# Neural codec with residual quantisation on one core: a tighter rule for which x transposes and which adding DMAs may be in flight together

## The chip, the cores and the metric

The kernel runs on one core of one Trainium2 chip. The metric is the device time of one execution in microseconds. The kernel before took 708.34 us in the median of three runs (700.25 to 710.99).

## The reference

The input x has 2 sequences of 16000 tokens with 512 channels, in bf16. A depthwise convolution with 3 taps over time and a SiLU give z. Then four codebooks of 8 words each quantise z in turn, each on what the one before has left over. The sum of the chosen words goes through a second depthwise convolution with 3 taps.

```python
xp = jnp.pad(x, ((0,0),(pad,pad),(0,0)))
for i in range(K):
    z = z + xp[:, i:i+T, :] * dw_enc[i][None, None, :]
z = _silu(z)
res = z
for s in range(Nq):
    cb = codebooks[s]
    d2 = |res|^2 - 2.0 * einsum("btd,cd->btc", res, cb) + |cb|^2
    sel = cb[d2.argmin(-1)]
    q = q + sel
    res = res - sel
...
    y = y + qp[:, i:i+T, :] * dw_dec[i][None, None, :]
```

## The kernel before

The 32000 tokens stand as 128 partitions of 250 tokens. They are worked in 16 chunks of up to 16 token positions each (`SIZES`). For a chunk the work is done with channels on the partitions, so x has to be transposed: chunk 0 is transposed by TensorE, and each of the 15 others by five DMA transposes, issued on SyncE (SP) by `run` at L544. Four of them bring four positions each and the last one two; the last chunk has four of them and one single row, `edge` at L550. That makes 75 transposes. They fill `XT`, which has two buffers, so a chunk's transposes can begin when the chunk two before has been read for the last time.

In `front`, each of four channel blocks of a chunk makes three products of `XT` with a tap on VectorE (DVE, L614): one into `Z` (four buffers), two into `T` (four buffers). The products have to be summed. For the chunks after the first, `DMA_ADDS` says that the first sum of every block and the second sum of the last block are made by a DMA that adds `T` into `Z` (`total`, L620), issued on GpSimd (POOL); DVE makes the other sums (L622). That makes 15 x 5 = 75 adding DMAs. When an add has landed, its `T` buffer is free for a later product, and `Z` may be summed further or go to the exponential on ScalarE (ACT, L626). SiLU follows as exponential, plus one, logarithm, exponential and product.

The stages after that (scores on TensorE, maxima and keys on DVE, the choice, the new residue) and the decoder do not change. A finished block of output leaves as `YSB` (three buffers) by a DMA on SP (L908), so the stores and the transposes share one queue of instructions.

The order of everything is set beforehand by a planner (`Plan`): it simulates the engines with estimated costs and emits the instructions of all engines in one order. Its "DMA" engine issues one transfer at a time and may delay a change between the two kinds (`APART`, `CLUMP`). Each engine then works through its own instructions in that order and waits at semaphores. Beside the waits that the data ask for, `keep_apart` adds one to each transpose and to each add: a transpose waits for the landing of the last but one add emitted before it, and an add for that of the last but one transpose (`LAG = 2`). The plan does not know of these waits.

In the order of emission the transposes (R) and the adds (A) stand like this:

```
RRRRRRRARARAARARAARARRRARAAARRRARARRARAARRAARARRRARAAARAR
RRARAAARARRRAARAARARRARARAAARRRRAARAARARRRAARAARARRAARARA
RARRRARAAARARARARARARARRRRAAAAAAAAAA
```

Of the kernel before, what the change touches and what calls it, by code (L numbers as in the profile page):

```python
# [57 lines left out]
LAG = 2  # L58
# [151 lines left out]
def kernel(  # L210
# [181 lines left out]
    def pair_rows(s):  # L392
        pst = psA.tile([P, 2, 512], F32, name="ps_p", tag="psa")
        for k, src in ((0, CBC), (1, CB4)):
            nc.tensor.matmul(pst[:, k, :], lhsT=PICK[k][:, s, :, :, :].rearrange("p h a b -> p (h a b)"), rhs=src[0:NC, :],
                             start=True, stop=True)
        nc.scalar.activation(HIGH[s], pst[:, 0, :], ACT.Copy, scale=-1.0)
        nc.scalar.activation(EVEN[s], pst[:, 1, :], ACT.Copy, scale=-1.0)
# [21 lines left out]
    for name, first, tap, count in (("A0", 0, 1, 2), ("A1", 0, 0, 3), ("A2", 1, 0, 3), ("A3", 2, 0, 2),  # L420
                                    ("B0", 3, 0, 1), ("B3", 0, 2, 1), ("A2LO", 1, 0, 1)):
        t = const.tile([P, D], BF16, name=name)
# [35 lines left out]
    for s in range(Nq - 1):  # L458
        t = plan.add("ACT", 1.1, 1.5, [picked, clamped, book], early + 3.0 + s, lambda s=s: pair_rows(s), take=("psA",), give=("psA",))
# [1 line left out]
    codes.append(plan.add("DVE", 1.4, 1.6, [codes[0]], 0.1 * PERIOD, lambda: code_columns(RESB[1])))  # L461
    gate, decoder = [], []
    staged = [*words, scored[1], taps_in]
    runs, adds = [], []

    def keep_apart(t, mine, others):
        if len(others) >= LAG:
            tc.add_manual_dep(t.ins, others[-LAG].name, mybir.DependencyInfo(mybir.DependencyClass.Sync, mybir.DependencyReason.DATA),
                              reason="transposes and adds take turns")
        mine.append(t.ins)  # L470

# [59 lines left out]
    def load(st, org):  # L531
# [10 lines left out]
        def run(n, m):  # L542
            g = g0 + n - 1
            t = nc.sync.dma_start_transpose(out=st["XT"][:, n:n + m, :, :].rearrange("p n i t -> p (n i) t"),  # L544
                                        in_=xv[:, g:g + m, :].rearrange("p g d -> p (g d)"))
            keep_apart(t, runs, adds)

        def edge(n):
            st["XE"] = const.tile([P, KT, P], BF16, name="XE")
            keep_apart(nc.sync.dma_start_transpose(out=st["XE"], in_=group_rows(0)), runs, adds)  # L550
# [35 lines left out]
    def front(st, org):  # L586
# [19 lines left out]
        def block(i):  # L606
# [10 lines left out]
            def total(k):  # L617
                z, t = u["Z"][:, 0:G, :], u["ZTU"[k]][:, 0:G, :]
                if i in DMA_ADDS[st["n"]][k - 1]:
                    keep_apart(nc.gpsimd.dma_start(out=z, in_=t, accum_op=ALU.add), adds, runs)  # L620
                else:
                    nc.vector.tensor_tensor(out=z, in0=z, in1=t, op=ALU.add)  # L622
# [380 lines left out]
```

## Time and profile before

| | |
|---|---|
| median of three runs | 708.34 us (700.25 to 710.99) |
| profiled execution, its own time | 703.44 us |
| its span, first to last instruction | 701.6 us |
| mean granted TensorE clock | 0.952 |
| busy: PE / DVE / ACT / POOL | 572.6 / 628.1 / 616.2 / 85.5 us |
| DMA queue of SP (transposes, stores) | 69.61 MB, 45.9% of 16 engines' span |
| DMA queue of POOL (adds) | 39.76 MB, 32.3% |
| an add, issue to landing, median | 6.0 us |
| a transpose, issue to landing, median | 6.6 us |

A busy time is that of an engine's own work; an instruction that only issues a DMA does not count as work on SP. A line of a group gives the line of the kernel, the engine, the operation, what is written and read, the number of instructions, then the busy time with the mean of one, then the idle time of the engine just before them and what ended it. SPq and POOLq are the queues' own issuing and waiting. A wait for several semaphores is put down to the one that came last.

### The profile page before, as it was taken

Reading aid. Unit: us, or ns where it says so; the run is one execution under the profiler, and the core shown is the slowest. Engines: PE = TensorE matmul, PEld = TensorE weight load, DVE = VectorE, ACT = ScalarE, POOL = GpSimd, SP = SyncE. Lnnn points to the kernel's source line nnn. Section 1 sums busy time; section 2 is a strip of 40 time slices with the busy share of each in tenths; the row PEclk is TensorE's granted clock in tenths of the full one; section 3 lists DMA queues with packets and bytes.
Section 4 is the critical chain, followed back from the end, with each engine's and each line's share of the span. In section 5 each row is a group of like instructions: output and inputs, shape, how many; then the busy total and the mean of one; then the engine's idle time right before and its main releaser. Section 6 shows DMA issues by size and latency. Waiting matters only on the chain. (4 is left out here: it accounts for less than half of the span.)

```text
span 701.6 us, 25642 instructions
## 1 busy us (share of the span) xinstructions
PE 572.6 (82%) x11501; PEld 328.9 (47%) x11582; DVE 628.1 (90%) x1292; ACT 616.2 (88%) x519; POOL 85.5 (12%) x120
## 2 busy tenths in 40 slices
PE   5136778898988988899929788898989987999995
PEld 5023444454545545445515444464545554565552
DVE  8999999999999999999939799999999999968640
ACT  2789999999999999999939888999999999963567
POOL 6021111100101111101101111010112002000000
PEclk8559999999999999999979989999999999999999
DMA  7999997997797999799999959979998536210235
GB/s 161 155 179 169 159 174 154 183 215 144 174 175 177 168 215 187 174 172 185 158 81 199 183 104 182 183 183 184 189 171 174 143 92 163 78 66 33 82 141 230
DMA packets 160840, 111.27 MB, mean 159 GB/s; under 512 B 142425, under 2 KB 142810, under 8 KB 160602
## 3 DMA queue, kind: packets, MB, share of 16 engines
q1 hardware_dynamic: 148976, 69.61, 45.9%
q0 software_dynamic: 11472, 39.76, 32.3%
q8 instruction: 90, 1.47, 0.9%
q10 hardware_dynamic: 282, 0.26, 0.1%
q14 instruction: 20, 0.16, 0.1%
HBM read 2.39 MB, written 32.77 MB: 50 GB/s over the span
## 5 line engine op out<-in xcount | busy, mean ns | idle before, releaser
L710 PE MATMUL PS<-RES 128*64 128x72 bf16 (+1 forms) x8064 | 173.5, 201 | 30.5 <-DVE RES L314 16.7
L710 PEld LDWEIGHTS <-RES 128*64 128x64 bf16 x8064 | 168.8, 113 | 39.0 <-DVE RES L642 18.4
L846 DVE TENSOR_TENSOR RES<-RES,SEL 128x2048 bf16<-128x2048 bf16 (+1 forms) x135 | 153.6, 1152 | 7.0 <-PE SEL L836 6.4
L864 ACT ACTIVATE RES<-NEW 128x1024 bf16<-128x1024 f32 x114 | 118.9, 1075 | 23.2 <-PE NEW L857 22.9
L904 ACT ACTIVATE YSB<-Y 128x1024 bf16<-128x1024 f32 (+1 forms) x126 | 126.6, 1052 | 14.1 <-issue 3.6
L620 POOL DMA_DIRECT2D Z<-T x75 | 72.3, 968 | 494.9 <-DVE V L753 51.2
L626 ACT ACTIVATE E<-Z 128x2048 bf16<-128x2048 bf16 (+1 forms) x64 | 123.2, 1927 | 7.6 <-DVE Z L622 3.2
L634 ACT ACTIVATE LN<-E 128x2048 f32<-128x2048 bf16 (+1 forms) x64 | 123.9, 1936 | 6.5 <-DVE E L630 6.4
L637 ACT ACTIVATE E<-LN 128x2048 bf16<-128x2048 f32 (+1 forms) x64 | 123.6, 1931 | 0.2
L614 DVE TENSOR_SCALAR T<-XT,WENC 128x2048 bf16<-128x2048 bf16 (+1 forms) x128 | 93.7, 738 | 20.8 <-DMA Z<-T 20.1
L730 DVE TENSOR_REDUCE TR<-PS 128x6 bf16<-128x384 f32 (+1 forms) x188 | 94.2, 507 | 18.4 <-PE PS L710 18.2
L852 PE MATMUL NEW<-RES,IDENT 128*128 128x512 bf16 (+1 forms) x252 | 76.4, 386 | 17.5 <-DVE RES L846 10.7
L898 PE MATMUL Y<-A,OHT 128*128 128x512 bf16 x205 | 74.5, 383 | 11.7 <-ACT YSB L904 3.3
L642 DVE TENSOR_TENSOR RES<-Z,E 128x2048 bf16<-128x2048 bf16 (+1 forms) x64 | 76.7, 1198 | 0.6 <-PE PS L710 0.4
L702 PE MATMUL PS<-MASK,IDENT 128*64 128x384 bf16 (+1 forms) x376 | 63.0, 331 | 5.5 <-DVE PR L734 3.4
L622 DVE TENSOR_TENSOR Z<-Z,T 128x2048 bf16<-128x2048 bf16 (+1 forms) x53 | 62.3, 1176 | 2.3 <-DMA Z<-T 2.3
L836 PE MATMUL SEL<-PH,HIGH 64*128 64x512 bf16 (+1 forms) x258 | 51.0, 389 | 15.9 <-ACT RES L864 5.8
L857 PE MATMUL NEW<-PH,EVEN 64*128 64x256 bf16 (+1 forms) x252 | 53.4, 420 | 0.0
L898 PEld LDWEIGHTS <-OHT 128*128 128x128 bf16 x373 | 31.7, 98 | 43.4 <-issue 16.9
L857 PE MATMUL NEW<-PH,HIGH 64*128 64x256 bf16 (+1 forms) x252 | 49.4, 388 | 2.9 <-ACT PH L809 2.9
L836 PE MATMUL SEL<-PH,LOW 64*128 64x512 bf16 (+1 forms) x258 | 49.3, 373 | 0.0
L836 PE MATMUL SEL<-PH,MID 64*128 64x512 bf16 (+1 forms) x258 | 49.2, 373 | 0.0
(111 smaller groups left out, 591.3 us busy)
## 6 DMA issues: line engine op xcount, KB each, us to landing
Z<-T POOLq DMA_DIRECT2D x75, 512.0 KB, 6.0
out_dram<-YSB SPq DMA_DIRECT2D x61, 512.0 KB, 4.5
RES<-in_x_dram SPq DMA_DIRECT2D x1, 1664.0 KB, 6.8
XT<-in_x_dram SPq DMA_TRANSPOSE x74, 6.6
out_dram<-YSB SPq DMA_DIRECT2D x1, 384.0 KB
out_dram<-YSB SPq DMA_DIRECT2D x1, 256.0 KB, 2.9
A<-in_dw_dec_dram POOLq DMA_DIRECT2D x2, 96.0 KB, 9.6
CB<-in_codebooks_dram ACTq DMA_DIRECT2D x1, 128.0 KB
```

The costliest lines, as they stand in the source:

```text
L614: nc.vector.tensor_scalar(out=places(u[name]), in0=taps(i, k), scalar1=WENC[:, i, k:k + 1], scalar2=None, op0=ALU.mult)
L626: nc.scalar.activation(u["E"][:, 0:G, :], u["Z"][:, 0:G, :], ACT.Exp, scale=-1.0)
L634: nc.scalar.activation(u["LN"][:, 0:G, :], u["E"][:, 0:G, :], ACT.Ln)
L637: nc.scalar.activation(u["E"][:, 0:G, :], u["LN"][:, 0:G, :], ACT.Exp, scale=-1.0)
L710: nc.tensor.matmul(V[d * HT:(d + 1) * HT, own - left:own + HT + right], lhsT=row[:, at:at + HT], rhs=row[:, at - left:at + HT + right], st ...
L730: nc.vector.tensor_reduce(out=to, in_=both(u["V", q], m, home, HT), axis=AX.X, op=ALU.max)
L836: nc.tensor.matmul(SEL[:, h, 0:W], lhsT=words[side(h), i * P:(i + 1) * P], rhs=u["PH"][side(h), :], start=(k == 0), stop=(k == len(parts) ...
L846: nc.vector.tensor_tensor(out=old, in0=old, in1=new, op=ALU.add)
L857: nc.tensor.matmul(odd[:, h, k, 0:W // 2], lhsT=words[side(h), i * P:(i + 1) * P], rhs=pairs[side(h)], start=False, stop=True, skip_group_ ...
L864: nc.scalar.activation(old, new.rearrange("p h (n t) -> p (h n) t", t=HT), ACT.Copy)
L898: nc.tensor.matmul(Y[:, h, :], lhsT=lhs(), rhs=rhs, start=(a == 0), stop=(a == len(terms) - 1))
L904: nc.scalar.activation(u["YSB"][:, k:k + n, :], u[k][:, 0:n, :], ACT.Copy)
```

## The change

`keep_apart` now remembers which kind came last. The first transpose after an add still waits for the last but one add, and the first add after a transpose for the last but one transpose. Each further one of the same kind in a row waits for the last of the other kind. Thus of the 75 + 75 waits, 24 of transposes and 30 of adds now name a transfer that is one later. The plan, the order on each engine and all other waits are as before.

```diff
-    runs, adds = [], []
+    runs, adds, turns = [], [], []
 
     def keep_apart(t, mine, others):
-        if len(others) >= LAG:
-            tc.add_manual_dep(t.ins, others[-LAG].name, mybir.DependencyInfo(mybir.DependencyClass.Sync, mybir.DependencyReason.DATA),
+        lag = LAG if turns[-1:] == [id(others)] else 1
+        turns.append(id(mine))
+        if len(others) >= lag:
+            tc.add_manual_dep(t.ins, others[-lag].name, mybir.DependencyInfo(mybir.DependencyClass.Sync, mybir.DependencyReason.DATA),
                               reason="transposes and adds take turns")
         mine.append(t.ins)
```

## The prediction

> **What bounds the kernel now.** I read the page first: busy shares, the slices, then the two groups that the change can reach.
>
> ```profile
> span 701.6 us, 25642 instructions
> PE 572.6 (82%) x11501; PEld 328.9 (47%) x11582; DVE 628.1 (90%) x1292; ACT 616.2 (88%) x519; POOL 85.5 (12%) x120
> DVE  8999999999999999999939799999999999968640
> ...
> L620 POOL DMA_DIRECT2D Z<-T x75 | 72.3, 968 | 494.9 <-DVE V L753 51.2
> ...
> L614 DVE TENSOR_SCALAR T<-XT,WENC 128x2048 bf16<-128x2048 bf16 (+1 forms) x128 | 93.7, 738 | 20.8 <-DMA Z<-T 20.1
> ```
>
> VectorE (DVE) is busy nine tenths of every slice but the ends and one hole: slice 21 of 40, about 351 to 368 us, is at 3. The product L614 idles 20.8 us, and 20.1 of it ends on an adding DMA. Next, DVE's waits between 31 and 600 us (engine, line, releaser: sum, times, longest), then two stages of the table by stage (us; busy of PE, PEld, DVE, ACT, POOL; granted clock; DMA share; GB/s).
>
> ```profile
> DVE T L614 <- DMA Z<-T: 20.1, 6, 12.6
> DVE TR L730 <- PE PS L710: 2.8, 7, 0.8
> DVE Z L622 <- DMA Z<-T: 2.3, 3, 1.0
> ...
> 210.00:300.00 90.00, 79.67 (x1696) 46.10 (x1707) 88.72 (x182) 87.89 (x75) 11.43 (x13) 1.00 0.88 183
> ...
> 345.00:370.00 25.00, 12.66 (x275) 7.66 (x271) 12.43 (x25) 14.31 (x11) 0.86 (x1) 0.80 0.98 92
> ```
>
> So an undisturbed stage runs DVE at 88.72 of 90 us. What DVE loses in mid-kernel it loses to adds that land late: 20.1 + 2.3 = 22.4 us in nine waits. All other waits there are small. The DMA share in the bad stage is 0.98 at half the usual GB/s: the engines were occupied and moved little.
>
> **The change part by part.** No instruction is added, removed or reordered; only what a transpose (SP, L544) or an add (POOL, L620) waits for. In the sequence shown above, 54 waits move on by one member: 24 transposes and 30 adds, each the second or later of its row. I number both kinds from 0.
>
> *The adds' 30 new waits.* Each is for the last transpose of the row before, when one for the last but one is already met. In the profiled order those transposes left long before the add did, so I cost these at nothing. The cover is the earlier add of the row, at 968 ns of issue, and the products that DVE makes between the two; without it, each would cost what a late transpose costs below.
>
> *The hole.* Timeline rows (start, length, engine) around it, then time to landing of the add at 343.67 and of the transpose at 348.12, then the same over all adds from 31 to 343 us and from 370 to 600 us:
>
> ```profile
> 343.19 4.88 SPq L544 DMA_TRANSPOSE XT<-in_x_dram  x1
> 343.67 0.86 POOL L620 DMA_DIRECT2D Z<-T  x1 [5.38 <-DVE PR L734]
> 348.12 14.29 SPq L544 DMA_TRANSPOSE XT<-in_x_dram  x1
> 362.76 0.75 DVE L614 TENSOR_SCALAR T<-XT,WENC 128x2048 bf16<-128x2048 bf16 x1 [12.57 <-DMA Z<-T]
> ...
> DMA to landing us min/median/max: 19.1/19.1/19.1
> DMA to landing us min/median/max: 16.6/16.6/16.6
> ...
> DMA to landing us min/median/max: 4.5/6.0/8.3
> DMA to landing us min/median/max: 4.5/6.4/9.3
> ```
>
> Add 44 is issued 0.48 us behind transpose 51; transpose 52, second in its row, joins at 348.12. The add takes 19.1 us, and DVE, ready at 362.76 - 12.57 = 350.19, stands until it lands, for want of a T buffer. After the change transpose 52 waits for add 44. Bounds for the add beside transpose 51 alone: 6.0 us (median) to 9.3 (longest elsewhere), so it lands between 349.7 and 353.0 and DVE waits 0 to 2.8 us: a saving of 9.8 to 12.57. Lower bound: no saving, if transpose 51 alone did it (a rival below). I take 11, since every other add with a transpose beside it stays inside 9.3.
>
> *Two smaller stalls.*
>
> ```profile
> 393.12 1.47 POOL L620 DMA_DIRECT2D Z<-T  x1 [6.93 <-DVE PR L734]
> 393.96 6.65 SPq L544 DMA_TRANSPOSE XT<-in_x_dram  x1
> 400.90 0.75 DVE L614 TENSOR_SCALAR T<-XT,WENC 128x2048 bf16<-128x2048 bf16 x1 [4.92 <-DMA Z<-T]
> ...
> 197.81 0.75 DVE L614 TENSOR_SCALAR T<-XT,WENC 128x2048 bf16<-128x2048 bf16 x1 [1.45 <-DMA Z<-T]
> ```
>
> Transpose 57 (393.96), third of its row, comes right behind add 49 (393.12). Without it the add lands at 6.0 us, 399.1, not 400.9: saves 1.8 (0 to 3.3, by the 4.5 minimum). At 197.81 the third-in-row transpose only started as the add landed: nothing. The remaining waits, 22.4 - 12.57 - 4.92 - 1.45 = 3.5 us, have one transpose or none beside them: nothing.
>
> *What the waiting transposes cost.* Eight of the 24 had not been clear of the add by the profile: numbers 13, 27, 37, 46, 52, 57, 62, 72. The others left when that add was down or within half a us of it. First and last of the eight, each behind its add:
>
> ```profile
> 71.52 0.86 POOL L620 DMA_DIRECT2D Z<-T  x1 [6.61 <-DVE PR L734]
> 72.87 5.77 SPq L544 DMA_TRANSPOSE XT<-in_x_dram  x1
> ...
> 516.60 0.86 POOL L620 DMA_DIRECT2D Z<-T  x1 [6.12 <-DVE MT L791]
> 520.92 2.57 SPq L544 DMA_TRANSPOSE XT<-in_x_dram  x1
> ```
>
> With the 6.0 us median the first waits 71.52 + 6.0 - 72.87 = 4.65 us, the last 1.7; the eight together about 25 us, or 25 + 8 x 3.3 = 51 with the longest landing, 9.3. Little of this is lost. DMA packets, us 234 to 236.5 (an add, q0, beside a transpose, q1), then 238 to 241 (transposes alone):
>
> ```profile
> q0 software_dynamic: 129, 0.47, 94.3%
> q1 hardware_dynamic: 142, 0.03, 6.2%
> ...
> q1 hardware_dynamic: 2607, 0.65, 98.5%
> ```
>
> While the add's data moves, transposes get 142 / 2.5 = 57 packets a us; alone 2607 / 3 = 869. A transpose that waits its turn gives up a fifteenth of its speed. What it truly loses is the start from landing to first packet, once per place.
>
> Then, who waits for it. On SP the stores stand behind it; on POOL the next row's first add, which waits for the last transpose but one; on DVE the first product of the chunk. SP's waits, POOL's wait, the last transpose of a chunk (418.65, 8.5 to landing) with that chunk's first product, and add 29, transpose 37 and the add behind it:
>
> ```profile
> SPq L908 <- ACT YSB L904: 165.3, 35, 16.6
> SPq L544 <- DMA Z<-T: 95.9, 23, 9.5
> POOL Z L620 <- DMA XT<-in_x_dram: 14.9, 3, 11.6
> ...
> 418.65 4.85 SPq L544 DMA_TRANSPOSE XT<-in_x_dram  x1
> DMA to landing us min/median/max: 8.5/8.5/8.5
> 433.59 0.74 DVE L614 TENSOR_SCALAR T<-XT,WENC 128x2048 bf16<-128x2048 bf16 x1
> ...
> 230.31 0.86 POOL L620 DMA_DIRECT2D Z<-T  x1 [5.16 <-DVE E L630]
> 233.37 4.65 SPq L544 DMA_TRANSPOSE XT<-in_x_dram  x1
> 242.04 0.86 POOL L620 DMA_DIRECT2D Z<-T  x1 [10.87 <-DVE V L753]
> ```
>
> SP sits idle 165.3 us for output tiles, so stores have cover. This chunk lands at 418.65 + 8.5 = 427.2 and is first read at 433.59: 6.4 us of slack, more than the 5.2 us of the longest single wait. The adds are the thin place. Transpose 37 would leave at 230.31 + 6.0 = 236.3, or at 238.6 with the 8.3 us of the longest landing up to then; with 4.65 us of issue it is done by 243 or so, against 242.04 for the add behind it: 1 us late. I take 1 us for all such places together (the other waits end before DVE's inputs for the add are ready). Bounds: -1, if freed adds also start sooner, to 25, if every wait reaches DVE.
>
> *The sum.* On the profiled execution, 703.44 us (span 701.6 and 1.8 around it): - 11 - 1.8 + 1 = - 11.8, so 691.6. That execution lies 4.9 below the median of 708.34 (runs 700.25 to 710.99). I take the median run to carry more of the same stalls and let half of the 4.9 stay: 691.6 + 2.4 = 694.
>
> A rule of the Trainium skill speaks against the 11: in "DMA: Bandwidth & Descriptors", section "Queues, rings and completion order", each DMA engine takes turns between its queues packet by packet. By it a second transpose in the same queue takes no extra turns from the add, and the sum would lose its first term and most of its second: about 704. The rows at 234 us agree with it (142 packets beside 129); the hole, where one add took 19.1 us, does not look like it.
>
> **The rivals.**
>
> *The stall stays.* What slowed add 44 is transpose 51, ahead of it since 343.19 and still allowed beside it. For it: DMA was already slow before 348.12 (110 GB/s from 346 to 349), and in the queues transpose 52 stands behind 51. Against it: most other adds have one transpose beside them and none exceeds 9.3 us. Then only the 1.8 goes and 1 comes: 702.6, or nothing gained if a stall falls elsewhere: 702, up to 708.
>
> ```profile
> 346.00:349.00 3.00, 3.00 (x84) 1.86 (x79) 3.00 (x9) 3.00 (x4) 0.00 (x0) 1.00 1.41 110
> 349.00:362.00 13.00, 3.06 (x71) 1.81 (x65) 1.19 (x2) 5.53 (x5) 0.00 (x0) 0.81 1.20 65
> ```
>
> *Slower: transposes held behind adds hold the next adds.* One chain: add lands, transpose leaves, next row's add waits for it, DVE waits for that add. It decides where a transpose's new wait exceeds the add's room, about 1 us at the place above. If the eight waits, 25 us, reach DVE and the savings stand: 691.6 + 25 = 717, and 720 with the 2.4. For it: 23 transpose waits on adds already exist, and POOL lost 14.9 us to transposes. Against: the speeds of 57 and 869 above, and 6.4 us at the chunk's edge.
>
> *All the add stalls go.* If relief shortens every late add, DVE's 22.4 us vanish: 703.44 - 22.4 + 2.4 = 683.
>
> *It does nothing.* 46 of 54 waits are already met; if the other eight also sit inside slack and the hole is chance, the time is that of before, 703 to 708. I put it with the first rival.
>
> **How the numbers follow.** No change cannot be told from a difference under about 2% here, so the lines are 694.2 and 722.5. Forecast 694: chance 0.48, its own range 687 to 700, just over half of it (0.25) below 694.2. Stall stays or nothing: 0.22, 702 to 708. Slower: 0.18, 709 to 735, two thirds (0.12) above 722.5. All stalls go: 0.12. Faster by over 2%: 0.25 + 0.12 = 0.37. Slower: 0.12. Within: the remaining 0.51. The range 684 to 712 leaves out half of the last case and most of the slower one, together under 0.2.
>
> **What would show it.** Right: the longest L620 time to landing falls from 19.1 to under 10, DVE's L614 wait on adds falls from 20.1 us to about 8, the DMA-starved slice 21 fills, and SP's L544 waits on adds rise from 95.9 us by about 25. Wrong: an add still takes over 12 us with only one transpose beside it (the stall stays), or POOL's waits on transposes and DVE's on adds both grow (slower).

## The result: 0.7% slower, and the profile after

Over 20 runs each, the changed kernel takes 710.66 us in the median (706.57 to 716.56), the kernel before 706.87 (700.25 to 716.74). The ratio is 1.0068, with a 95% interval of 1.0042 to 1.0094: 3 to 7 us slower, where 14 us faster had been forecast. Executions more than 1.5% above the fastest of their kernel are left out of the ratios and their intervals here and below, so a ratio differs a little from the quotient of the medians (here 1.0054). The profiled execution after took 707.11 us, before 703.44.

The page after, its lines that answer to those of before (line numbers of the changed part are two higher):

```profile
span 705.3 us, 25642 instructions
PE 578.1 (82%) x11501; PEld 332.0 (47%) x11582; DVE 629.1 (89%) x1292; ACT 616.8 (87%) x519; POOL 86.3 (12%) x120
...
DVE  8999998999989999999939799999999999868640
...
L616 DVE TENSOR_SCALAR T<-XT,WENC 128x2048 bf16<-128x2048 bf16 (+1 forms) x128 | 93.9, 740 | 19.7 <-DMA Z<-T 19.7
```

The hole in DVE is where it was, slice 21 at 3. DVE's waits between 31 and 600 us say the same (sum, times, longest):

```profile
DVE T L616 <- DMA Z<-T: 19.7, 4, 12.9
DVE Z L624 <- DMA Z<-T: 4.2, 3, 3.2
```

19.7 + 4.2 = 23.9 us against 22.4 before. The stall is as deep as ever, although its suspect is gone. The rows of the timeline around it (start, length, engine), with the time to landing of the add:

```profile
344.79 4.90 SPq L546 DMA_TRANSPOSE XT<-in_x_dram  x1
345.28 0.86 POOL L622 DMA_DIRECT2D Z<-T  x1 [5.38 <-DVE PR L736]
364.72 2.20 SPq L546 DMA_TRANSPOSE XT<-in_x_dram  x1
364.73 0.75 DVE L616 TENSOR_SCALAR T<-XT,WENC 128x2048 bf16<-128x2048 bf16 x1 [12.94 <-DMA Z<-T]
...
DMA to landing us min/median/max: 19.4/19.4/19.4
```

Transpose 52 now leaves at 364.72, after the add has landed, as the change wants it. Still add 44 takes 19.4 us, 0.49 us behind transpose 51, and DVE stands 12.94 us. So transpose 52 is not needed for the stall.

The waits of the two DMA queues between 31 and 600 us, SP on adds and POOL on transposes:

```profile
SPq L546 <- DMA Z<-T: 148.8, 35, 15.0
...
POOL Z L622 <- DMA XT<-in_x_dram: 34.5, 3, 18.0
```

SP waits 53 us more (95.9 before; 25 more had been forecast), of which 15.0 is transpose 52 at the stall. POOL's waits that end on a transpose grew from 14.9 to 34.5 us. That is a sign that adds are held behind transposes that leave later, but no measure of it: a wait counts the whole idle time of the engine, put down to what came last. One such add, number 65, before and after:

```profile
530.14 0.86 POOL L620 DMA_DIRECT2D Z<-T  x1
```

```profile
526.49 1.40 SPq L546 DMA_TRANSPOSE XT<-in_x_dram  x1
...
534.20 0.86 POOL L622 DMA_DIRECT2D Z<-T  x1
```

Transpose 72, which left at 520.92 before, now waits for add 64 and leaves at 526.49. The single row that transpose 73 brings comes later with it, POOL's copy of that row stands ahead of add 65 in POOL's queue, and the add leaves 4.1 us later. Of this, 2.1 us had piled up by add 64 (516.60 before, 518.66 after), so the hold itself is 2.0 us.

### The profile page after: what moved, and what is told of

Read it like the earlier page. It is cut to its first block, busy times and chain, and to the rows that moved or that the text cites. A ratio compares the mean times of both kernels' runs of the same rounds, so it can differ in the third digit from the quotient of the medians.

```text
span 705.3 us, 25642 instructions
## 1 busy us (share of the span) xinstructions
PE 578.1 (82%) x11501; PEld 332.0 (47%) x11582; DVE 629.1 (89%) x1292; ACT 616.8 (87%) x519; POOL 86.3 (12%) x120
## 5 line engine op out<-in xcount | busy, mean ns | idle before, releaser
L712 PE MATMUL PS<-RES 128*64 128x72 bf16 (+1 forms) x8064 | 176.0, 202 | 28.3 <-DVE RES L314 15.7
L712 PEld LDWEIGHTS <-RES 128*64 128x64 bf16 x8064 | 171.6, 115 | 36.8 <-DVE RES L644 17.5
L906 ACT ACTIVATE YSB<-Y 128x1024 bf16<-128x1024 f32 (+1 forms) x126 | 126.3, 1047 | 14.9 <-issue 3.6
L616 DVE TENSOR_SCALAR T<-XT,WENC 128x2048 bf16<-128x2048 bf16 (+1 forms) x128 | 93.9, 740 | 19.7 <-DMA Z<-T 19.7
L854 PE MATMUL NEW<-RES,IDENT 128*128 128x512 bf16 (+1 forms) x252 | 78.0, 392 | 18.2 <-DVE RES L848 12.2
L838 PE MATMUL SEL<-PH,HIGH 64*128 64x512 bf16 (+1 forms) x258 | 51.6, 393 | 16.2 <-ACT RES L866 6.2
```

The lines of the kernel that those rows point to most:

```text
L616: nc.vector.tensor_scalar(out=places(u[name]), in0=taps(i, k), scalar1=WENC[:, i, k:k + 1], scalar2=None, op0=ALU.mult)
L712: nc.tensor.matmul(V[d * HT:(d + 1) * HT, own - left:own + HT + right], lhsT=row[:, at:at + HT], rhs=row[:, at - left:at + HT + right], st ...
L838: nc.tensor.matmul(SEL[:, h, 0:W], lhsT=words[side(h), i * P:(i + 1) * P], rhs=u["PH"][side(h), :], start=(k == 0), stop=(k == len(parts) ...
L906: nc.scalar.activation(u["YSB"][:, k:k + n, :], u[k][:, 0:n, :], ACT.Copy)
```

## The experiments

Two questions: where do the 4.8 us come from, and what makes the stall, if not transpose 52? In the diffs, `again` is true for a transpose or an add that follows one of its own kind, and `len(mine)` is the number of the transfer in its kind's order, counted from 0. Each diff shows only the line that sets the wait, in place of that of the changed kernel, with the experiment's short name as a comment; `LAG` alone is the wait of the kernel before. In e7, which has that wait throughout, the lines of the store are shown. Each kernel was timed beside the kernel before on the same chip.

### Which half of the change costs

```diff
-        lag = LAG if turns[-1:] == [id(others)] else 1
+        lag = 1 if again and mine is runs else LAG      # e1: transposes only
```

> Only the 24 transpose waits of the change, the adds wait as before. If the slowdown comes from transposes held behind adds, which then hold the next row's first add: the ratio to the kernel before is that of the whole change, 1.004 to 1.010, SP's waits of transposes on adds between 31 and 600 us stay near 149 us (before 96), and adds 12, 30 and 65 leave late as in the changed kernel. If instead the adds' 30 waits cost the time: ratio 1.000. The hole (add 44, 19 us to landing) stays by either theory.

Measured: ratio 1.0061 (1.0020 to 1.0102). SP's waits on adds are 143.7 us, and add 44 takes 17.6 us.

```diff
+        lag = 1 if again and mine is adds else LAG      # e2: adds only
```

> Only the 30 add waits of the change, the transposes wait as before. If the transposes' waits are the cause: ratio 1.000 within its interval and SP's waits of transposes on adds near 96 us. If the adds' waits are the cause: 1.004 to 1.010. The hole stays by either theory.

Measured: ratio 0.998 (0.9943 to 1.0017). SP's waits on adds are 96.9 us; add 44 takes 16.3 us. So the 24 waits of the transposes are the cost, and the 30 of the adds cost nothing that can be told.

The adds that were to leave late do so. Microseconds from the start of the add that a row of transposes waits for to the start of the add behind that row (e9, further below, has the transposes' waits, but adds that wait for a much earlier transpose):

| | before | after | e1 | e2 | e9 |
|---|---|---|---|---|---|
| add 11 to add 12 | 13.4 | 14.3 | 15.6 | 13.5 | 9.8 |
| add 29 to add 30 | 11.7 | 13.1 | 13.0 | 11.6 | 11.5 |
| add 64 to add 65 | 13.5 | 15.5 | 15.5 | 13.7 | 15.5 |

With the transposes' waits and the old add waits (after and e1) these adds are held 1 to 2 us longer than before. POOL's waits that end on a transpose are 17.0 us in e1, hardly more than the 14.9 before, although e1 costs as much as the whole change; so the 34.5 us above are not the size of the loss.

### No overlap at all, and one pair apart

```diff
+        lag = 1                                         # e3
```

> Every transpose waits for the last add before it and every add for the last transpose before it: none of them overlap. Theory pair (the hole is one transpose beside one add): no add takes over 10 us to land, the hole of 12.6 us is gone, but some 50 more waits of 2 to 6 us lie on adds: 700 to 725 us. Theory event (the hole belongs to that add or that moment, whatever is beside it): one add still takes about 19 us, and the time is 715 to 740 us.

Measured: 788.06 us, ratio 1.1158 (1.1087 to 1.1230). The stall is gone (median landing 5.7 us), but one add still takes 11.5 us, against the forecast of under 10: add 22, with no transpose in flight and two stores issued 0.5 and 1.4 us behind it. The price is far above both forecasts. DVE's and POOL's waits in this kernel, over the whole span:

```profile
DVE Z L625 <- DMA Z<-T: 61.5, 23, 6.1
...
DVE T L617 <- DMA Z<-T: 19.1, 7, 7.8
```

```profile
POOL Z L623 <- DMA XT<-in_x_dram: 117.5, 12, 13.7
```

POOL's waits that end on a transpose are 117.5 us (14.9 before), and DVE waits 61.5 + 19.1 = 80.6 us for adds (22.4 before), 58 us more in a kernel that is 82 us slower. Taking turns strictly makes every transfer a link of one chain. In this run the adds land no later than before (5.7 us in the median, 6.0 before), which points to adds that leave late as the loss, and not to adds that are slow.

```diff
+        lag = 1 if mine is runs and len(mine) == 51 else LAG     # e4
```

> The kernel before with one wait changed: transpose 51 waits for add 44 instead of add 43. Theory pair: add 44 lands in 6 to 9 us, DVE's 12.6 us stall at 363 us shrinks to 0 to 3 us, and the time falls by 9 to 12 us, ratio 0.983 to 0.988. Theory event: add 44 (or a neighbour) still takes about 19 us, ratio 1.000.

Measured: 693.28 us, ratio 0.9843 (0.9796 to 0.9891). One wait out of 150 is worth 12 us. Its rows: the add, its time to landing, transpose 51, and the product that stood 12.57 us:

```profile
342.90 0.86 POOL L623 DMA_DIRECT2D Z<-T  x1 [5.38 <-DVE PR L737]
...
DMA to landing us min/median/max: 6.3/6.3/6.3
...
349.25 2.35 SPq L547 DMA_TRANSPOSE XT<-in_x_dram  x1
...
349.33 0.75 DVE L617 TENSOR_SCALAR T<-XT,WENC 128x2048 bf16<-128x2048 bf16 x1
```

The add lands after 6.3 us, the product follows without a wait, and transpose 51 leaves 6 us later; the next stall on an add is 2.35 us, at 368 us. So the stall needs transpose 51 beside add 44.

### What is bad about this pair

Other pairs stand 0.5 us apart, and their adds land in 6 to 9 us (add 29 in 8.2, add 54 in 8.1). Two things looked special: the exact start, and an output store that SP issues just before transpose 51.

```diff
+        lag = 1 if mine is adds and len(mine) == 44 else LAG     # e6
```

> The kernel before with add 44 waiting for transpose 50 instead of 49: it starts a little later (by up to 2 us), transpose 51 still beside it. If the bad pair is a coincidence of a fixed start 0.5 us apart: add 44 lands in under 10 us, ratio 0.983 to 0.990. If it belongs to these two transfers whatever their exact start: over 15 us to landing, ratio 0.998 to 1.004.

Measured: 698.20 us, ratio 0.9849 (0.9790 to 0.9909). Transpose 51, the add, its time to landing, the product (the line numbers are smaller because blank lines are left out of this kernel):

```profile
350.40 4.30 SPq L531 DMA_TRANSPOSE XT<-in_x_dram  x1
...
352.91 1.31 POOL L606 DMA_DIRECT2D Z<-T  x1 [7.40 <-DVE V L738]
...
DMA to landing us min/median/max: 7.5/7.5/7.5
...
360.44 0.75 DVE L600 TENSOR_SCALAR T<-XT,WENC 128x2048 bf16<-128x2048 bf16 x1 [3.04 <-DMA Z<-T]
```

The add starts 2.5 us behind the transpose instead of 0.5 and lands in 7.5 us, with the same transpose beside it.

```diff
+            stored.append(g)
+            if len(stored) != 20:                       # e7
                 nc.sync.dma_start(out=outv[...], in_=u["YSB"][...])
```

> The kernel before without the output store that SP issues between transposes 50 and 51 (one of 64 stores, 512 KB, is left out, so that part of the output is not written). If the stall needs the store as a third party in the queues: add 44 lands in under 10 us and the ratio is 0.982 to 0.988. If the pair alone does it: still over 15 us, ratio 0.998 to 1.002.

Measured: 692.05 us, ratio 0.9757 (0.9707 to 0.9807). Transpose 51, the add and its time to landing:

```profile
345.48 3.79 SPq L547 DMA_TRANSPOSE XT<-in_x_dram  x1
...
345.98 0.86 POOL L623 DMA_DIRECT2D Z<-T  x1 [5.39 <-DVE PR L737]
...
DMA to landing us min/median/max: 7.0/7.0/7.0
```

The pair stands 0.50 us apart, just as in the kernel before (0.48), and the add lands in 7.0 us. Without the store there is no stall. So the store of 340.41, the transpose of 343.19 and the add of 343.67 are each needed here. Transpose 50, issued 2.2 us ahead of the store, is the same in all these runs, so whether it is needed too was not tested. The ratio is lower than that of e4 and than the forecast; the left-out store is itself less to move, so only the landing is read from this run.

### Does the change cost the same without the stall, and through what

```diff
+        lag = 1 if again or (mine is runs and len(mine) == 51) else LAG     # e5
```

> The whole change, and also transpose 51 waits for add 44. If the stall and the late adds are separate terms that add up: the ratio is that of the single pair times that of the change, 0.9843 x 1.0068 = 0.991 (0.986 to 0.996). If the change's waits cost only because they interact with the stall: 0.984 as with the single pair alone. Add 44 lands in under 10 us.

Measured: 699.75 us, ratio 0.9847 (0.9800 to 0.9893). The sum of terms, 0.991, lies just outside, 0.984 inside. The two intervals, of e4 and e5, are each half a per cent wide to either side, so this does not show that the cost vanishes. The profiled executions speak against it: e5's took 696.96 us and e4's 692.07, 4.9 us apart, which is the cost of the change again; but that is one execution of each.

```diff
+        lag = 4 if mine is adds else 1 if again else LAG         # e9
+        lag = 4 if mine is adds else LAG                         # e10
```

> The change's 24 transpose waits, but an add waits for the fourth last transpose, which has landed long before, so no late transpose can hold an add. If the change costs time by holding adds: the ratio to the kernel before falls from 1.0061 (transpose waits alone) to that of the next kernel, without the change and with free adds, within 0.3%. If late transposes cost time in another way (x late for DVE, transposes colliding with the next add): it stays 0.5% or more above the next kernel.

> The kernel before with adds that wait for the fourth last transpose. Adds 12 and 14 are no longer held 4 us, so if holding adds costs: ratio 0.993 to 0.998. If the adds' old wait keeps them out of a worse overlap: 1.003 or more, with longer landings than the 6.0 us median. The stall at add 44 stays (12.6 us), since its wait does not bind.

Measured: e9 0.9986 (0.9946 to 1.0026), e10 0.9966 (0.9932 to 1.0001). With free adds the change's waits cost 0.2%, within the noise, where they cost 0.61% with the old add waits. Within one chip the medians say the same: e9 703.50 and e10 703.85 us, no cost; e1 709.18 and e2 704.73, 4.5 us. In e9 SP waits nearly as long as in the changed kernel, and POOL's list has no wait of an add on a transpose left. All of SP's and POOL's waits on DMAs between 31 and 600 us:

```profile
SPq L547 <- DMA Z<-T: 138.1, 34, 11.8
```

```profile
POOL Z L623 <- DMA Z<-T: 4.8, 1, 4.8
```

So late transposes by themselves cost nothing that these runs can tell, and late transposes that hold an add are the likely cost. One add is held in e9 all the same, number 65, by POOL's copy of the single row (15.5 us behind add 64, in the table above); it costs nothing visible. DVE's wait behind add 12 fits: 1.0 us before, 3.2 after, 3.0 in e1, 3.1 in e5, none in the four kernels with free adds. But in the five kernels with neither the change's 24 waits nor free adds (e2, e4, e6, e7, e8) it ranges from 0 to 2.9 us, so one profile of each does not fix the place of the loss. Add 44 stalls on in both (16.2 and 17.5 us to landing).

### The way to a faster kernel

```diff
+        lag = 1 if mine is runs and len(mine) in (51, 56) else LAG          # e8
```

> The kernel before with two waits changed: transpose 51 waits for add 44, transpose 56 for add 49, behind which DVE stood 4.9 us. If one transpose beside an add is harmful in general: add 49 lands in 4.5 to 6 us instead of 7.8, DVE's stall there falls from 4 to 5 us to 1 to 3, ratio 0.979 to 0.983. If only the pair 51 and 44 is: 0.984, no better than that pair alone, since transposes 56 to 59 come later.

Measured: 695.59 us, ratio 0.9758 (0.9694 to 0.9821). This interval overlaps that of e4, so the second wait's own gain is not settled by the times. Its rows show the gain: add 49 lands in 5.6 us instead of 7.8, and DVE behind it stands 2.27 us instead of 4.92:

```profile
387.62 0.89 POOL L623 DMA_DIRECT2D Z<-T  x1 [6.43 <-DMA Z<-T]
...
DMA to landing us min/median/max: 5.6/5.6/5.6
...
393.24 0.75 DVE L617 TENSOR_SCALAR T<-XT,WENC 128x2048 bf16<-128x2048 bf16 x1 [2.27 <-DMA Z<-T]
```

```diff
+        lag = 4 if mine is adds else 1 if len(mine) in (51, 56) else LAG    # e11
+        lag = 4 if mine is adds else 1 if again or len(mine) in (51, 56) else LAG   # e12
```

> The free adds, and transposes 51 and 56 wait for adds 44 and 49. If the three terms add up: 0.976 less whatever free adds gain, 0.970 to 0.975. If free adds run into worse overlaps: 0.98 or more.

> The whole set of transpose waits of the change, free adds (they wait for the fourth last transpose), and transposes 51 and 56 waiting for adds 44 and 49. If keeping second transposes away from adds is worth something once no add is held: ratio 0.965 to 0.972, below the 0.975 of the same kernel without the change's waits. If it is worth nothing: 0.973 to 0.978. If late transposes still cost: 0.98 or more.

Measured: e11 689.05 us, ratio 0.9750 (0.9709 to 0.9791); e12 690.07 us, 0.9758 (0.9701 to 0.9814). Both are 2.4 to 2.5% faster than the kernel before. Free adds gain nothing over the two pairs alone (e8, 0.9758) that can be told from noise, and neither do the change's own waits where adds are free.

## Why the prediction was wrong, point by point

- *What bounds the kernel.* Right. DVE has few gaps in mid-kernel but for late adds, and taking one of those stalls away moved the time by its full size: 12.57 us of stall, and 12.4 us of median in e4.
- *The adds' 30 new waits at nothing.* Right: e2, 0.998 (0.9943 to 1.0017).
- *The hole, 11 us.* This step failed. It named transpose 52 because its 14.29 us of issue overlap the add's 19.1 us. That long issue was a victim of the stall, not its cause: with the transpose held back, the add took 19.4 us (17.6 in e1, 16.2 in e9). The step had argued that other adds with one transpose beside them stay within 9.3 us, which holds where that trace has a landing (66 of the 75 adds), and that therefore the second transpose made the difference. It had not asked what else stood in the queues. Two stores of the kernel before, the one with an empty queue and the one just before transpose 51:

```profile
299.94 0.33 SPq L908 DMA_DIRECT2D out_dram<-YSB  x1
...
340.41 2.69 SPq L908 DMA_DIRECT2D out_dram<-YSB  x1
```

The second, 2.69 us in issue, was the third party, and its long issue was a row to look at. So the 11 us stood on the wrong transfer. That a stall of this size could be had was right, and its size was near: e4 gained 12.4 us by holding the other transpose.
- *Two smaller stalls, 1.8 us.* About half: 4.92 to 3.95 us at add 49, and 1.45 to 1.77 at the other. The change still allows transpose 56 beside the first; with that held too (e8) the stall is 2.27.
- *What the waiting transposes cost, 1 us.* The way was right as far as the runs show, the size too small: the change costs 4.8 us (3 to 7) by its ratio, and e1 puts it on these waits. At the one place that was priced the estimate was good: add 30 leaves at 246.17 where it was 242.04, but add 29 is itself 2.8 us later (233.08, before 230.31), so the hold is 1.4 us. What was missed are holds that the sum put at nothing. Add 12 leaves 0.9 us further behind add 11; it stands behind transpose 17, which was not among the eight, as it left within half a us of add 11's landing. Add 65 leaves 2.0 us further behind add 64. Taking 6.0 us for every landing was low as well: seven of the eight adds took 6.0 to 8.0 us after the change, and one 19.4. Transpose 37 and add 30 after:

```profile
239.73 2.12 SPq L546 DMA_TRANSPOSE XT<-in_x_dram  x1
...
246.17 0.93 POOL L622 DMA_DIRECT2D Z<-T  x1 [12.23 <-DVE RES L644]
```

- *The rivals.* "The stall stays", given 0.22 and 702 to 708 us, is what happened on the profiled execution, 707.11; the median, 710.66, lies above its bound, as the waits' cost came on top. Its reason, transpose 51, was half of the truth. The rule of the Trainium skill that each DMA engine takes turns between its queues by packet ("DMA: Bandwidth & Descriptors", "Queues, rings and completion order") gave 704 and the right verdict on transpose 52. It does not give the stall itself: by it one transpose and one store in SP's queue should cost the add no more than a packet at a time. "Slower: transposes held behind adds hold the next adds" happened as well, as far as e9 and e10 show it, at about a fifth of its price, 4.8 us of 25. (Its sum, 691.6 + 25 + 2.4, is 719 and not 720.)
- *The median run.* Half of 4.9 us was added for a median above the profiled execution. Over 20 runs the median of before is 3.4 us above it, so this term was of the right order.

What stays open: why a store, a transpose and an add, all started within 3.3 us, collapse to a fraction of the usual rate, while other such groups do not. Add 39 of the changed kernel, for one, leaves at 303.96 with a transpose 0.5 us and a store 2.0 us ahead of it, and lands in 6.8 us; that store's issue took 0.33 us where the one at the stall took 2.69. The runs show that the store and the transpose are each needed at add 44 and that 2 us of distance is enough. They do not show that every long landing has this cause: in e8 and e11 add 34, between two transposes and with no store issued in the 7.9 us before it, took 12.0 and 11.3 us. Which of the engines or memories gives way was not shown either.

## What to carry to other kernels

When a transfer takes three times its usual time, list everything in flight at its start, those that began earlier in the same queue included, before blaming the one that overlaps it longest; a transfer that is itself stretched may be a victim. An order rule for all transfers can cost at each of them, through whatever waits next in turn, while the loss sat in one place: changing one wait of 150 gained 12 us, changing 54 lost 5. Before adding a wait, follow it one link further than its own instruction: here SP's queue had room for it (its stores wait 147.2 us for output tiles), and the price most likely stood on the other queue.

## What the runs showed of the hardware

- An add that starts within 3.3 us of a store and a transpose can take 19 us in place of 6 to 7; the same add with the transpose 2 us further ahead, with the transpose held, or with the store left out, does not. In the stall, from 350 to 364 us of the changed kernel, the DMA share is 0.85 at 51 GB/s:

```profile
350.00:364.00 14.00, 4.07 (x101) 2.54 (x98) 1.79 (x4) 6.54 (x5) 0.00 (x0) 0.78 0.85 51
```

- In the stall the packets themselves are slow. In the kernel before, from 349 to 356 us, the 838 packets of SP's queue took 83.9% of 16 engines' 7 us, which is 0.112 us each; the 2607 packets of transposes alone, from 238 to 241 us, took 98.5% of 16 engines' 3 us, 0.018 us each:

```profile
q1 hardware_dynamic: 838, 0.21, 83.9%
```

- The stall is not a chance event: it sits at the same add in all six profiled kernels that leave the three together (before, after, e1, e2, e9 and e10), with 16.2 to 19.4 us to landing. In all six the transpose starts 2.8 us behind the store and the add 0.5 us behind the transpose. Three of them hold transpose 52 back (19.4, 17.6 and 16.2 us) and three do not (19.1, 16.3 and 17.5).
- TensorE's granted clock falls with it, 0.78 in this stretch, in which the engine is busy for 4.07 of 14 us; before it, from 347 to 350 us, when it is busy all the time, it is 1.00.
